# Conversion of float64 weights to float32 in a retention layer with two FFNs: the low word as an integer of 0 to 8, added to the high word's bits

## Chip, cores and metric

The kernel runs on one core of a Trainium2 chip. The metric is the device time of one launch in microseconds. The kernel before takes 1128.92 us, the median of three runs (1128.47 to 1130.82).

## What is computed

A retention layer over 4 x 8 heads, 768 tokens and 64 features, then an FFN with a quadratic gate, then an FFN whose two inputs are multiplied. The weights arrive as float64 and are used as float32.

```python
state = gamma * state + k_t v_t^T          # per head, 768 steps
x     = scale * q_t state                  # 3072 x 512 after all heads are laid side by side
h     = x @ w_in                           # 512 x 2048
g     = where(h >= 1, h, where(h <= -1, 0, (h + 1)**2 / 4))
x     = g @ w_out                          # 2048 x 512
out   = ((x @ w1) * (x @ w2)) @ w3 @ w_out2    # 512 x 1024, 512 x 1024, 1024 x 1024, 1024 x 512
```

## The kernel before

Tokens are worked on in 6 tiles of 512. The retention goes by 24 chunks of 128 tokens, each in four pieces (`piece_mm`, `piece_ew`): two of scores (`a_t`), one for the state, one for the output, which is split into `xh` and `xl`, the float32r halves that the first FFN reads. The first four chunks (16 pieces) run before the first FFN; the others run ahead of it, two pieces per slot at first, none in slots 7 to 18, then about one.

The first FFN has 96 slots (`SLOTS`), one for each token tile and block f of 128 hidden features. The first two tiles take the first half of the blocks, then the second half. A slot is `emit_h` (12 matmuls of 512 columns: high by high, low by high, high by low, over four blocks of the contraction), `emit_g1` (Relu and Square on ScalarE, a max-min on VectorE, into `r`), from slot 11 on `emit_g2` (split of `r` into `gh`, `gl`) and `emit_wo` (split of the `w_out` block into `wo_s`), and `emit_y1` one slot later. Slots 0 to 10 (`PLAIN`) use `r` and `wo_f` unsplit in plain float32. A split is a copy on ScalarE and a subtraction on VectorE (L96, L97). The product `w3 @ w_out2` and the second FFN follow; they read converted weights back from DRAM.

Weights are loaded as raw pairs of words (`load_job`, L118, on SP's DMA queue, 2 `raw` buffers), and become float32 in `converter`. `magnitude` (L155) takes the absolute value of the high word on ScalarE. VectorE then clamps it (L171), shifts it left by three and masks it (L176), puts sign and top exponent bit back (L181), masks the result to its power of two (L186), multiplies that by the low word and 2^-52 (L190), and adds the two (L202 for `w_in`, L218 for `w_out`, L229 for what is spilled to DRAM). The work list: `w_in` block 0 and 1 in 512 columns each, then ten conversions of 1024 columns (two blocks each, `w_out` and `w_in` in turn), then, from slot 10 on, ten of 512 columns for the rest of both, and forty of 512 columns whose result is stored to DRAM (`done_spill`).

The order on each engine is the program's order, as written. A planner decides where conversion steps stand: it books the time of each engine in `now`, with a cost for each step (the numbers that `converter` yields) and a due time for what VectorE does next. Where VectorE would wait for a matmul, `dve` puts in conversion steps until they would pass the due time, or until the weights that they need would not have arrived (`now["conv"]`). `magnitude` of the next conversion and the load of the one after it are issued when the generator is resumed after its fifth step, with the first step of `done`. SP's queue also carries the q, k and v loads (`chunk_ahead`) and the stores of converted weights, in program order.

Of the kernel before, what the change touches and what calls it, by code (L numbers as in the profile page):

```python
# [9 lines left out]
F32 = mybir.dt.float32  # L10
F32R = mybir.dt.float32r
U32 = mybir.dt.uint32
AF = mybir.ActivationFunctionType
ALU = mybir.AluOpType

B, H, S, D = 4, 8, 768, 64
P = 128
# [15 lines left out]
NB = NTILE * NF2  # L33
AHEAD = 6
HALF = NF1 // 2
# slots of the first FFN: the first two tiles take the weights in two halves, as they arrive
SLOTS = [(i, f) for lo in (0, HALF) for i in (0, 1) for f in range(lo, lo + HALF)]
SLOTS += [(i, f) for i in range(2, NTILE) for f in range(NF1)]
PLAIN = 11
# [10 lines left out]
def retention_then_two_ffns(  # L50
# [17 lines left out]
    nc = tc.nc  # L68
# [22 lines left out]
    cpool = conversion.enter_context(tc.tile_pool(name="cpool0", bufs=2))  # L91
# [9 lines left out]
        nc.tensor.matmul(out=ps, lhsT=ll, rhs=rh, start=False, stop=False)  # L101
        nc.tensor.matmul(out=ps, lhsT=lh, rhs=rl, start=False, stop=last)  # L102

# [1 line left out]
    win = {}  # L105
    wo = {}
    spill = {}
# [21 lines left out]
        return now["pe"]  # L129

    def dve(cost, after=0.0):
        """Counts a step of VectorE; weights are converted while it would wait."""
        while (jobs or conv is not None) and len(jobs) + 1 > now["hold"]:
            if conv is None:
                load_job(jobs[0])
                now["conv"] = max(now["conv"], ready[("raw", jobs[0][2])] + 1.1)
            start = max(now["dve"], now["conv"])
            if start + (0.2 if now["slip"] else 0.8) > after:
                break
            run_conv(1)  # L140
        now["dve"] = max(now["dve"], after) + cost
        return now["dve"]

    def dma(size, after=0.0):
        """When a load of so many KB arrives."""
        now["dma"] = max(now["dma"], after) + size / 350.0
        return now["dma"] + 1.9

    magnitudes = {}

    def magnitude(job):
        load_job(job)
        _, n, key, _ = job
        u = cpool.tile([P, n], U32, tag="u", name="u")
        nc.scalar.activation(out=u.bitcast(F32), in_=raws[key][:, 1::2].bitcast(F32), func=AF.Abs)  # L155
        magnitudes[key] = u
        now["conv"] = ready[("raw", key)] + 1.1

    def converter():
        """Yields the time of each step that holds VectorE."""  # L160
        while jobs:
            job = jobs.popleft()
            _, n, key, done = job
            if key not in magnitudes:
                magnitude(job)
            now["dve"] = max(now["dve"], now["conv"])
            raw, u = raws.pop(key), magnitudes.pop(key)
            lo, hi = raw[:, 0::2], raw[:, 1::2]
            w = cpool.tile([P, n], F32, tag="wf", name="w_f")
            uf, wu = u.bitcast(F32), w.bitcast(U32)  # L170
            nc.vector.tensor_scalar(  # L171
                out=uf, in0=uf, scalar1=bits(0x38000000), scalar2=bits(0x47F00000),
                op0=ALU.max, op1=ALU.min,
            )
            yield 0.2 + n / 1920
            nc.vector.tensor_scalar(  # L176
                out=u, in0=u, scalar1=3, scalar2=0x3FFFFFFF,
                op0=ALU.logical_shift_left, op1=ALU.bitwise_and,
            )
            yield 0.2 + n / 1920  # L180
            nc.vector.scalar_tensor_tensor(  # L181
                out=wu, in0=hi, scalar=0xC0000000, in1=u,
                op0=ALU.bitwise_and, op1=ALU.bitwise_or,
            )
            yield 0.2 + n / 960
            nc.vector.tensor_scalar(  # L186
                out=u, in0=wu, scalar1=0xFF800000, scalar2=None, op0=ALU.bitwise_and
            )
            yield 0.2 + n / 1920
            nc.vector.scalar_tensor_tensor(  # L190
                out=uf, in0=lo, scalar=2.0 ** -52, in1=uf, op0=ALU.mult, op1=ALU.mult
            )
            yield 0.2 + n / 960
            if jobs:
                magnitude(jobs[0])
            if len(jobs) > 1:
                load_job(jobs[1])
            yield from done(w, uf)

    def done_win(f):  # L200
        def done(w, u):
            nc.vector.tensor_tensor(out=w, in0=w, in1=u, op=ALU.add)  # L202
            yield 0.2 + w.shape[-1] / 960
            for i in range(w.shape[-1] // 512):
                t = new_w("win")
                split(t[:, 0, :], t[:, 1, :], w[:, i * 512:(i + 1) * 512])
                win[f + i] = t
                ready[("win", f + i)] = now["dve"] + 0.8
                yield 0.73

        return done

    def done_wo(f):
        def done(w, u):
            for i in range(w.shape[-1] // 512):
                t = wpool.tile([P, 512], F32, tag="wo", name="wo_f")
                c0 = i * 512
                nc.vector.tensor_tensor(  # L218
                    out=t, in0=w[:, c0:c0 + 512], in1=u[:, c0:c0 + 512], op=ALU.add
                )  # L220
                wo[f + i] = t
                ready[("wo", f + i)] = now["dve"] + 0.8
                yield 0.73

        return done

    def done_spill(key):
        def done(w, u):
            nc.vector.tensor_tensor(out=w, in0=w, in1=u, op=ALU.add)  # L229
            d = dram.tile([P, 512], F32, name=f"sp_{key[0]}_{key[1]}")  # L230
            nc.sync.dma_start(out=d, in_=w)
            spill[key] = d
            yield 0.73

        return done
# [17 lines left out]
        while jobs or conv is not None:  # L253
            run_conv(1)

# [1 line left out]
    stream = deque()  # L257
    arrived = deque()

# [6 lines left out]

    wos = {}

# [1 line left out]
    ch = {}  # L270
    vt = {}
    kt = {}
# [131 lines left out]
        )  # L404

    def chunk_ahead(a):
        """Loads where PE has long been done with what was there, so that no other load waits."""
        g, part = divmod(a, PIECES)
        if a < TILE_PIECES:
            if part == 0 and g:  # L410
# [11 lines left out]
        elif part == 2:  # L422
            scale_chunk(g + 1)

# [1 line left out]
    hps = {}  # L426
    gs = {}
    y1acc = {}
# [49 lines left out]
    y1_st = {}  # L478

    def group(n):  # L480
        """The slots that are summed up in PSUM together."""
        i, f = SLOTS[n]
        lo, hi = (0, NF1) if i > 1 else (0, HALF) if f < HALF else (HALF, NF1)
        return i, f == lo, f == hi - 1, hi < NF1, lo > 0
# [48 lines left out]
            nc.sync.dma_start(out=(y1_part if partial else y1_d)[i][m], in_=st)  # L533
        dve(2.2 if more else 0.8)

# [1 line left out]
    wo2 = {}  # L537
    w3 = {}
    wc = {}
# [29 lines left out]
            split(hi, lo, ps)  # L569
            wc[4 * hf + i] = (hi, lo)  # L570

# [1 line left out]
    wab = {}  # L573
    yt = {}
    abps = {}
# [62 lines left out]
    with tc.manual_schedule():  # L638
        for i in range(2):
            nc.gpsimd.memset(kp[i], 0.0)  # L640
            nc.gpsimd.memset(vp[i], 0.0)
        # in the order in which the slots want them
        order = [("win", w_in, 0, done_win)]
        for f in range(2, NF1, 2):
            order += [("wo", w_out, f - 2, done_wo), ("win", w_in, f, done_win)]
# [19 lines left out]
        load_job(jobs[0])  # L665
        load_v(1)

        # the first tile of tokens, while the first weights arrive
        early = [jobs[1]]
        for a in range(TILE_PIECES):  # L670
            piece_mm(a)
# [2 lines left out]
                load_job(early.pop(0))  # L674
            piece_ew(a)

        # first FFN; the retention runs ahead of it
        todo = deque(range(TILE_PIECES, NSTEP))
        now["slip"] = True
        for n in range(-1, NA):  # L680
# [92 lines left out]
            if hf:  # L773
                load_ab(NF2 + j)

        # second FFN
        for n in range(NB):
            i, f = divmod(n, NF2)
            if n + 1 < NB:
# [76 lines left out]
```

## Time and profile before

| | |
|---|---|
| median of three runs | 1128.92 us |
| lowest and highest run | 1128.47, 1130.82 us |
| span of the profiled execution | 1128.7 us |
| TensorE matmul (PE) busy | 1103.3 us, 98% |
| VectorE (DVE) busy | 630.1 us, 56% |
| ScalarE (ACT) busy | 390.7 us, 35% |
| GpSimd (POOL) busy | 69.4 us, 6% |

All times inside an execution are microseconds from the span's start. The releaser behind an arrow is what ended the idle time in front of an instruction. Matmuls overlap: their pace is the distance of their starts, not the duration of one. Busy shares are means over stages with different limits, so the page's totals are only the start; the rows further down are from windows and timelines of single stages.

### The profile page before, as it was taken

What the parts mean: (1) busy time and instruction counts of PE and PEld (TensorE: products, weight loads), DVE (VectorE), ACT (ScalarE), POOL (GpSimd) and SP (SyncE); (2) the same over time, 40 slices, a digit from 0 to 9 for tenths busy, and PEclk for the clock granted to TensorE, in tenths of its full rate; (3) what the DMA queues carried; (4) which work ended last, traced back from release to release, by engine and by line L of the source; (5) the groups of instructions that cost most, each with busy time, mean ns of one, the idle gap of its engine ahead of it and who ended that gap; (6) DMA issues with size and microseconds to landing.
All of it is one profiled execution on the core that took longest, in us unless ns stands there. A gap on an engine that the chain in (4) does not pass through costs nothing.

```text
span 1128.7 us, 13282 instructions
## 1 busy us (share of the span) xinstructions
PE 1103.3 (98%) x5268; PEld 916.0 (81%) x5268; DVE 630.1 (56%) x968; ACT 390.7 (35%) x657; POOL 69.4 (6%) x55
## 2 busy tenths in 40 slices
PE   6889999999999999999999999999999999999998
PEld 6666578888888888888888888888888888888887
DVE  5888778888989898887444454432221212122211
ACT  1223355434444544444334564421121212122111
POOL 3300100111011011010000000000000000000000
PEclk9899999999999999999999999999999999999999
DMA  7544225355544454353103123410101101010101
GB/s 207 178 159 152 90 94 172 99 185 179 177 150 150 137 170 160 131 160 111 38 1 131 47 84 112 137 60 1 66 10 45 30 1 66 1 38 0 38 1 38
DMA packets 56462, 107.37 MB, mean 95 GB/s; under 512 B 5584, under 2 KB 18000, under 8 KB 55120
## 3 DMA queue, kind: packets, MB, share of 16 engines
q1 hardware_dynamic: 56400, 106.52, 29.2%
q8 instruction: 41, 0.67, 0.3%
q14 instruction: 21, 0.17, 0.0%
HBM read 81.33 MB, written 25.17 MB: 94 GB/s over the span
## 4 chain that ended last, share of the span: by engine, by line
PE 93%; DVE 3%; DMA 2%; ACT 1%; POOL 1%; issue 0%; SPq 0%; POOLq 0%
PE hps L102 8%; PE hps L101 8%; PE ab L102 8%; PE ab L100 8%; PE ab L101 8%; PE hps L100 8%; PE y1acc L101 7%; PE y1acc L100 7%; PE y1acc L102 7%; PE oacc L629 4%; PE oacc L627 4%; PE oacc L628 4%; PE pa L339 3%; PE pa L359 3%; PE y1acc L501 2%; PE w3acc L100 1%
## 5 line engine op out<-in xcount | busy, mean ns | idle before, releaser
L612 DVE TENSOR_TENSOR pr<-ab,pr 128x512 f32<-128x512 f32 x48 | 33.2, 692 | 269.2 <-PE ab L102 269.2
L100 PE MATMUL hps<-xh,win 128*128 128x512 f32 x384 | 153.9, 401 | 6.6 <-ACT win L96 5.1
L102 PE MATMUL hps<-xl,win 128*128 128x512 f32 x384 | 151.7, 395 | 2.9 <-DVE xl L402 2.9
L101 PE MATMUL hps<-xh,win 128*128 128x512 f32 x384 | 151.5, 395 | 0.7 <-DVE win L97 0.7
L100 PE MATMUL ab<-yh,wab 128*128 128x512 f32 x384 | 149.4, 389 | 0.0
L101 PE MATMUL ab<-yh,wab 128*128 128x512 f32 x384 | 149.4, 389 | 0.0
L102 PE MATMUL ab<-yl,wab 128*128 128x512 f32 x384 | 149.4, 389 | 0.0
L100 PE MATMUL y1acc<-gh,wo_s 128*128 128x512 f32 x340 | 137.2, 404 | 0.0
L449 ACT ACTIVATE r<-hps 128x512 f32<-128x512 f32 x96 | 57.4, 598 | 229.1 <-PE hps L102 229.1
L101 PE MATMUL y1acc<-gh,wo_s 128*128 128x512 f32 x340 | 132.7, 390 | 0.0
L102 PE MATMUL y1acc<-gl,wo_s 128*128 128x512 f32 x340 | 132.5, 390 | 0.0
L451 DVE SCALAR_TENSOR_TENSOR r<-hps,r 128x512 f32<-128x512 f32 x96 | 66.3, 690 | 115.3 <-ACT r L450 115.0
L100 PEld LDWEIGHTS hps<-xh,win 128*128 128x128 f32 x384 | 73.4, 191 | 23.2 <-ACT win L96 5.6
L102 PEld LDWEIGHTS hps<-xl,win 128*128 128x128 f32 x384 | 73.3, 191 | 19.0 <-DVE xl L402 3.8
L101 PEld LDWEIGHTS hps<-xh,win 128*128 128x128 f32 x384 | 73.2, 191 | 17.4 <-DVE win L97 1.6
L611 ACT COPY pr<-ab 128x512 f32<-128x512 f32 x48 | 28.2, 587 | 170.8 <-PE ab L102 170.8
L101 PEld LDWEIGHTS ab<-yh,wab 128*128 128x128 f32 x384 | 72.1, 188 | 15.1
L102 PEld LDWEIGHTS ab<-yl,wab 128*128 128x128 f32 x384 | 72.1, 188 | 14.9
L100 PEld LDWEIGHTS ab<-yh,wab 128*128 128x128 f32 x384 | 72.1, 188 | 14.9
L96 ACT CAST ph<-pr 128x512 fp32r<-128x512 f32 x48 | 29.9, 622 | 138.2 <-DVE pr L612 138.2
L627 PE MATMUL oacc<-wch,ph 128*128 128x512 f32 x192 | 74.7, 389 | 0.0
L628 PE MATMUL oacc<-wcl,ph 128*128 128x512 f32 x192 | 74.7, 389 | 0.0
(71 smaller groups left out, 1789.5 us busy)
## 6 DMA issues: line engine op xcount, KB each, us to landing
raw<-in_w_dram SPq DMA_DIRECT2D x16, 512.0 KB, 3.9
raw<-in_w3t_dram SPq DMA_DIRECT2D x16, 512.0 KB, 3.7
raw<-in_w_out_dram SPq DMA_DIRECT2D x14, 512.0 KB, 4.0
q_t<-in_qT_dram SPq DMA_DIRECT2D x24, 256.0 KB, 4.9
kp<-in_kT_dram SPq DMA_DIRECT2D x48, 128.0 KB, 4.8
v_t<-in_v_dram SPq DMA_DIRECT2D x24, 256.0 KB, 4.4
y_d<-y1st SPq DMA_DIRECT2D x24, 256.0 KB, 2.6
f<-y_d SPq DMA_DIRECT2D x24, 256.0 KB, 2.7
```

Source lines behind the costliest of these rows:

```text
L96: nc.scalar.copy(out=hi, in_=src)
L100: nc.tensor.matmul(out=ps, lhsT=lh, rhs=rh, start=first, stop=False)
L101: nc.tensor.matmul(out=ps, lhsT=ll, rhs=rh, start=False, stop=False)
L102: nc.tensor.matmul(out=ps, lhsT=lh, rhs=rl, start=False, stop=last)
L339: nc.tensor.matmul(out=ps[:, j * C:(j + 1) * C], lhsT=kp[g % 2][:, h // 2, h % 2, :], rhs=q_t[:, h // 2, :], start=True, stop=True,)
L359: nc.tensor.matmul(out=y, lhsT=vb[:, p, h:h + 2, :], rhs=a_t[:, 2 * (p % 2) + h, :], start=(c == 0 and h == 0), stop=(h == 1),)
L449: nc.scalar.activation(out=r, in_=hps[n], func=AF.Relu, bias=0.5, scale=0.5)
L451: nc.vector.scalar_tensor_tensor(out=r, in0=hps.pop(n), scalar=1.0, in1=r, op0=ALU.max, op1=ALU.min)
L612: nc.vector.tensor_tensor(out=r, in0=pb, in1=r, op=ALU.mult)
L627: nc.tensor.matmul(out=ps, lhsT=lh, rhs=wh, start=(f == 0), stop=False)
L628: nc.tensor.matmul(out=ps, lhsT=lh, rhs=wl, start=False, stop=False)
L629: nc.tensor.matmul(out=ps, lhsT=ll, rhs=wh, start=False, stop=(f == NF2 - 1))
```

## The change

`magnitude` becomes `tail`: besides the absolute value of the high word, ScalarE writes the low word, scaled by 2^-29 through a Relu, as an unsigned integer of 0 to 8. VectorE adds this integer to the shifted high word, where the float product and its mask stood, and the and-or with the sign bits (`join`) becomes the last step, in `done`, in place of the float sum. The tile `w_f` is gone; the finished weight of a spilled conversion lies in `u`, whose bytes the store reads. `tail` of the next conversion and the load of the one after it are issued after the third step of a conversion, ahead of `join`. The planner's costs follow the steps. Comments and docstrings go too; such hunks are left out here.

```diff
-    magnitudes = {}
-
-    def magnitude(job):
+    tails = {}
+
+    def tail(job):
+
         load_job(job)
         _, n, key, _ = job
         u = cpool.tile([P, n], U32, tag="u", name="u")
         nc.scalar.activation(out=u.bitcast(F32), in_=raws[key][:, 1::2].bitcast(F32), func=AF.Abs)
-        magnitudes[key] = u
+        r = cpool.tile([P, n], U32, tag="r", name="r")
+        nc.scalar.activation(out=r, in_=raws[key][:, 0::2], func=AF.Relu, scale=2.0 ** -29)
+        tails[key] = (u, r)
         now["conv"] = ready[("raw", key)] + 1.1
...
-            if key not in magnitudes:
-                magnitude(job)
+            if key not in tails:
+                tail(job)
             now["dve"] = max(now["dve"], now["conv"])
-            raw, u = raws.pop(key), magnitudes.pop(key)
-            lo, hi = raw[:, 0::2], raw[:, 1::2]
-            w = cpool.tile([P, n], F32, tag="wf", name="w_f")
-            uf, wu = u.bitcast(F32), w.bitcast(U32)
+            raw, (u, r) = raws.pop(key), tails.pop(key)
+            hi = raw[:, 1::2]
+            uf = u.bitcast(F32)
...
             yield 0.2 + n / 1920
-            nc.vector.scalar_tensor_tensor(
-                out=wu, in0=hi, scalar=0xC0000000, in1=u,
-                op0=ALU.bitwise_and, op1=ALU.bitwise_or,
-            )
-            yield 0.2 + n / 960
-            nc.vector.tensor_scalar(
-                out=u, in0=wu, scalar1=0xFF800000, scalar2=None, op0=ALU.bitwise_and
-            )
-            yield 0.2 + n / 1920
-            nc.vector.scalar_tensor_tensor(
-                out=uf, in0=lo, scalar=2.0 ** -52, in1=uf, op0=ALU.mult, op1=ALU.mult
-            )
+            nc.vector.tensor_tensor(out=u, in0=u, in1=r, op=ALU.add)
             yield 0.2 + n / 960
             if jobs:
-                magnitude(jobs[0])
+                tail(jobs[0])
             if len(jobs) > 1:
                 load_job(jobs[1])
-            yield from done(w, uf)
+            yield from done(hi, u)
+
+    def join(out, hi, u):
+
+        nc.vector.scalar_tensor_tensor(
+            out=out.bitcast(U32), in0=hi, scalar=0xC0000000, in1=u,
+            op0=ALU.bitwise_and, op1=ALU.bitwise_or,
+        )
 
     def done_win(f):
-        def done(w, u):
-            nc.vector.tensor_tensor(out=w, in0=w, in1=u, op=ALU.add)
+        def done(hi, u):
+            w = u.bitcast(F32)
+            join(w, hi, u)
             yield 0.2 + w.shape[-1] / 960
...
     def done_wo(f):
-        def done(w, u):
-            for i in range(w.shape[-1] // 512):
+        def done(hi, u):
+            for i in range(u.shape[-1] // 512):
                 t = wpool.tile([P, 512], F32, tag="wo", name="wo_f")
                 c0 = i * 512
-                nc.vector.tensor_tensor(
-                    out=t, in0=w[:, c0:c0 + 512], in1=u[:, c0:c0 + 512], op=ALU.add
-                )
+                join(t, hi[:, c0:c0 + 512], u[:, c0:c0 + 512])
...
     def done_spill(key):
-        def done(w, u):
-            nc.vector.tensor_tensor(out=w, in0=w, in1=u, op=ALU.add)
+        def done(hi, u):
+            w = u.bitcast(F32)
+            join(w, hi, u)
             d = dram.tile([P, 512], F32, name=f"sp_{key[0]}_{key[1]}")
             nc.sync.dma_start(out=d, in_=w)
```

## Rows read from the trace of the kernel before

**Rows 1.** The page's first part: busy time, share of the span, instructions.

```profile
PE 1103.3 (98%) x5268; PEld 916.0 (81%) x5268; DVE 630.1 (56%) x968; ACT 390.7 (35%) x657; POOL 69.4 (6%) x55
```

**Rows 2.** Windows: length, each engine's busy time, granted clock, DMA share, GB/s.

```profile
0.00:40.00 40.00, 28.13 (x184) 26.85 (x184) 25.40 (x37) 6.68 (x10) 12.26 (x15) 0.91 0.73 220
40.00:125.00 85.00, 75.31 (x340) 54.03 (x341) 71.28 (x85) 25.18 (x37) 15.14 (x10) 0.94 0.44 145
...
200.00:520.00 320.00, 320.00 (x1706) 275.57 (x1705) 284.06 (x465) 146.02 (x248) 34.75 (x25) 1.00 0.48 155
...
1000.00:1128.70 128.70, 124.84 (x551) 103.07 (x549) 26.14 (x39) 22.89 (x39) 0.00 (x0) 1.00 0.07 25
```

**Rows 3.** Timeline of PE, 40 to 125: start, duration; idle and releaser in brackets.

```profile
43.02 0.79 PE L102 MATMUL hps<-xl,win 128*128 128x512 f32 x1 [2.10 <-DVE xl L402]
...
59.41 0.50 PE L100 MATMUL hps<-xh,win 128*128 128x512 f32 x1 [0.85 <-ACT win L96]
...
79.71 0.50 PE L100 MATMUL hps<-xh,win 128*128 128x512 f32 x1 [2.72 <-ACT win L96]
...
100.36 0.50 PE L100 MATMUL hps<-xh,win 128*128 128x512 f32 x1 [1.50 <-ACT win L96]
...
119.69 0.50 PE L100 MATMUL hps<-xh,win 128*128 128x512 f32 x1 [0.88 <-ACT xh L397]
...
121.21 0.76 PE L102 MATMUL hps<-xl,win 128*128 128x512 f32 x1 [0.79 <-DVE xl L402]
```

**Rows 4.** Chain of waits, 60 to 83: start, its share of the chain, link.

```profile
61.10 0.23 PE hps L101
...
75.80 1.96 DVE u L190
77.78 1.24 DVE w_f L202
...
82.08 0.43 PE hps L101
```

**Rows 5.** Groups of VectorE by shape: count, busy time, mean ns, idle before.

```profile
L190 DVE SCALAR_TENSOR_TENSOR u<-raw,u 128x512 f32<-128x512 uint32 x52 | 40.7, 783 | 1.5
...
L186 DVE TENSOR_SCALAR u<-w_f 128x512 uint32<-128x512 uint32 x52 | 23.0, 443 | 1.2
...
L190 DVE SCALAR_TENSOR_TENSOR u<-raw,u 128x1024 f32<-128x1024 uint32 x10 | 13.7, 1372 | 0.3
L181 DVE SCALAR_TENSOR_TENSOR w_f<-raw,u 128x1024 uint32<-128x1024 uint32 x10 | 12.2, 1223 | 0.2
...
L186 DVE TENSOR_SCALAR u<-w_f 128x1024 uint32<-128x1024 uint32 x10 | 8.3, 834 | 0.2
```

**Rows 6.** Groups of ScalarE by shape: the absolute value over 1024 columns.

```profile
L155 ACT ACTIVATE u<-raw 128x1024 f32<-128x1024 f32 x10 | 11.5, 1146 | 10.3 <-DMA raw<-in_w_out_dram 10.3
```

**Rows 7.** Tile `raw`: 145 to 525 (three rows), then landing from 0 to 145.

```profile
L155 ACT ACTIVATE u<-raw x50: 652/672/684, 147.0 to 517.7; 128x512 f32<-128x512 f32 x50
...
  ACT u L155: 13.3, 9
...
DMA to landing us min/median/max: 3.2/3.8/6.1
...
DMA to landing us min/median/max: 3.4/4.8/6.5
```

**Rows 8.** DMA issues, 140 to 520: count, size, median us to landing.

```profile
sp_wab<-w_f SPq DMA_DIRECT2D x16, 256.0 KB, 4.0
```

**Rows 9.** Timelines of DVE, ACT, DVE and PE around one slot, 302 to 314.

```profile
302.97 0.68 DVE L97 TENSOR_TENSOR wo_s<-wo_f,wo_s 128x512 fp32r<-128x512 f32 x1
...
306.07 0.60 ACT L449 ACTIVATE r<-hps 128x512 f32<-128x512 f32 x1 [2.53 <-PE hps L102]
...
309.36 0.68 DVE L97 TENSOR_TENSOR wo_s<-wo_f,wo_s 128x512 fp32r<-128x512 f32 x1
...
313.03 0.48 PE L100 MATMUL y1acc<-gh,wo_s 128*128 128x512 f32 x1
```

## The prediction

> **What bounds the kernel now.** I read the page's engine totals first: TensorE is busy for 1103.3 of 1128.7 us [rows 1]. So the change, which takes nothing from TensorE, can win only what TensorE idles, 25.4 us, and what it loses to a lower granted clock. The table of windows shows where that lies [rows 2]: 11.87 us before 40 us, 9.69 us from 40 to 125, 3.86 in the last output tile; the row from 200 to 520 has PE busy for its whole length, and the remaining windows are like it. VectorE, whose work the change cuts, is 84% busy in the second stretch and 89% from 200 to 520. In the latter it costs nothing, since PE never waits there. The stretch that decides is therefore 40 to 125.
>
> Next, PE's timeline of that stretch with its idle times [rows 3]. 2.10 at 43.02 waits for `xl`, the subtraction of the last piece of the first token tile. 0.85, 2.72 and 1.50 wait for the split of freshly converted `win` weights. 0.88 and 0.79 at 119.7 and 121.2 wait for the copy and the subtraction that finish the second token tile. These add up to 8.84; the other 0.85 are small pieces, most of them right behind the three `win` gaps, where the second half of the same split is late. Then the chain of waits [rows 4]: ahead of the 2.72 stand the converter's own steps on VectorE, L190 and L202. And the same fp32r matmul, 0.23 us apart at 61 us, is 0.43 apart at 82 us, after that gap: the windows' granted clock is 0.94 over this stretch against 1.00 later. The timeline has eight such matmuls after each of the idle times at 43.0, 79.7 and 121.2, so each costs 8 x 0.20 = 1.6 us beside its idle time.
>
> **What is removed from VectorE.** Per conversion of 1024 columns: the mask L186, 0.83, and the scaled product L190, 1.37 [rows 5]; of 512 columns 0.44 and 0.78. The old sum (L202, L218, L229) stays in number: its place is taken by `join`, the and-or of L181, and L181's place by the integer addition. So 2.2 us go per large conversion and 1.22 per small one. Two large conversions belong to each pair of f blocks, and the pairs come about 20.3 us apart (59.41, 79.71, 100.36). VectorE gets back 4.4 of each 20.3 us, where PE was short of 2.72 and 1.50. In 40 to 125 that is eight conversions, 17.6 of the 71.28 busy us.
>
> **What is added to VectorE.** An integer addition of two dense tensors does not occur before. Its nearest rows: L181, two 32-bit streams, one of them strided, 1.22 for 1024 columns, and the slowest L190, 1.96 while GpSimd multiplied [rows 4, 5]. I take 1.22, as it is nearest in kind; at 1.96 the saving per conversion falls from 2.2 to 1.5, still 3.0 per pair. Below 1.22 I see no ground: a two-stream f32 addition is not cheaper in any row.
>
> **What is added to ScalarE.** One more pass per conversion, over the low words. Abs over the other strided half takes 1.15 for 1024 columns and 0.67 for 512 [rows 6, 7]; I take the same for Relu, since both read one strided word and write a dense one. From integer words it might be a little longer; with 1.5 and 1.0 as the top nothing below changes. ScalarE is busy 25.18 of 85 us in the stretch and 146 of 320 later [rows 2], so the time itself is covered by idle time. Its place in the queue is not.
>
> The rule of the Trainium skill that speaks against this is in "ScalarE: Activation LUTs", section "Rules for kernel authors": relu, multiplications and additions belong on VectorE, which is faster per element. By it the low word would be one VectorE pass, an estimated 0.83 to 1.37 per conversion, and the gain per conversion would shrink from 2.2 to about 1. In this trace the strided ScalarE pass, 1.15, is no longer than L190, and ScalarE has the free time; the row decides for the change.
>
> **What moves.** `tail(jobs[0])` and `load_job(jobs[1])` come after the third step instead of the fifth, and *before* `join`, which is now the last reader of `raw`. The load of conversion k+2 reuses the buffer of k and therefore waits on SP's queue for join(k). So do the q, k and v loads and the spill store behind it; in the early stretch the converter as a whole is 2.2 us shorter, so they leave earlier than now. `u` now carries the finished weight, so Abs of k+2 must also wait for the spill store of k (4.0 us to land [rows 8]); before, only the third VectorE step of k+2 waited for such a store (in `wf`). ScalarE works in order: while that Abs waits, the first FFN's Relu, Square and splits stand behind it.
>
> **The sum, early stretch.** With 4.4 us back per pair the conversions of `win` run ahead of PE, so the three `win` gaps go: 0.85 + 2.72 + 1.50, plus 0.6 of the small pieces, plus the 1.6 of clock at 80 us. Even if VectorE kept its present order, the pair due at 59.4 would finish 2.2 us earlier. At 121 the subtraction would no longer stand behind late weights: 0.79 and 1.6 of clock go; the 0.88 for the copy, which can start only when the piece is done, stays. At 43.0, VectorE's queue ahead of `xl` is shorter, but `tail` may now hold ScalarE ahead of the copy `xh`; I take 0.5 of 2.10 and leave the clock. Before 40 us GpSimd and the q loads end last, not VectorE: 0, with +-0.7 for the same ScalarE order. Sum: 0.85 + 2.72 + 1.50 + 0.6 + 1.6 + 0.79 + 1.6 + 0.5 = 10.2 us.
>
> **The charge from 145 us on.** Here PE has no gap to win, and it can only get some. 50 small conversions take 371 us [rows 7], at 6.39 us a slot (the two `wo_s` rows, 302.97 and 309.36 [rows 9]) 0.86 per slot. The planner books 3.6 us for one now (three steps of 0.47, three of 0.73) and 2.4 after, so it will place about 1.25 per slot: in a quarter of some 40 slots two `tail`s fall into one VectorE stretch between `wo_s` and `r`. Then the second Abs waits. The stretch starts behind `wo_s` at 303.6, 2.5 us before h ends, which is where Relu starts, 306.07 [rows 9]. join(k) is done 0.7 later, the load is issued and lands 3.8 after [rows 7], the store at 4.0 plus 0.7 of queue; ScalarE then needs 0.67 twice. Relu of the slot would start 3.6 to 4.2 us after h's end instead of at once. From Relu to the last split takes 4.0 now (306.07 to 310.04), and y1 is due 7.0 after h's end (313.03, all [rows 9]). So such a slot stalls PE 0.6 to 1.2 us; where the pair lies earlier in the stretch, not at all. I take 0.3 for 10 slots, 3 us, between 0 and 12.
>
> The profiled span, 1128.7, is the median of the three runs, 1128.92, within 0.2 us, so nothing is to be added around it. 1128.9 - 10.2 + 3.0 = 1121.7 us.
>
> **The rivals.**
> - *No charge.* The planner spaces the loads well, or the slack of 3 us holds. For it: PE has no gap after 125 us although Abs already waits for loads there. 1118.7; with all 9.69 idle and 4.8 of clock won, 1114.4.
> - *Half the gain.* ScalarE, held ahead of `xh` by a `tail` that waits for its load (large loads land 4.8 after issue, up to 6.5 [rows 7]), makes new gaps of 2 to 3 us with their 1.6 of clock at the two tile starts. Against: the planner moves conversions away from there. -5 + 3: 1126.9.
> - *Slower.* The charge decides: same mechanism, but half of 40 slots pay the full 1.2 us, 24 us. 1128.9 - 10.2 + 24 = 1142.7. It turns the sign from 0.25 us per small conversion on. Against: it needs two tails in one stretch in every second slot, and the planner makes a conversion wait for its load.
> - *The change does not do what it says*: the new addition always runs at the slowest row, 1.96, and VectorE is relieved by a third less. A pair still gets 3.0 back against a gap of 2.72, so this costs some 1 us more: 1122.7.
>
> **How the numbers follow.** The forecast, 1119.5 to 1125, gets 0.50; no charge 0.23; half the gain 0.14; slower 0.11; nothing at all 0.02. The range takes in the first three and the unknown prices, and cuts the best end and the slower rival: 1116 to 1129. This kernel's measurement can tell 0.2% (2.3 us) from no change. Faster by more than that: forecast and no charge, 0.73. Within it: half the gain and nothing, 0.15. Slower: 0.12.
>
> **What would show it.** In the changed profile: no `win` gap over 0.5 us between 55 and 105 us; 0.23 us spacing at the matmuls that follow; VectorE busy in 40 to 125 near 54 us. For the charge: Abs waiting for `raw` or for a spill store for more than the 13.3 us of now [rows 7], and PE idle between 145 and 450 behind `gh` or `wo_s`, 0 to 12 us. The last small conversion starts near 400 us instead of 517.7. I am wrong if the gaps stay with VectorE idle before them (then a load or ScalarE holds the weights), or if PE idles after 145 us by more than 10 us.

## The result, and the profile after

The changed kernel takes 1145.3 us, the median of four runs (1140.77 to 1148.8), against 1128.81 for the kernel before in the same comparison: a ratio of 1.0135, 95% interval 1.0104 to 1.0166. It is slower by 1.35%, where 1121.7 and faster was forecast, and it lies above the range of 1116 to 1129. The profiled execution has a span of 1145.5 us.

Part 1 of the page and the windows of the changed kernel (length, then each engine's busy time, granted clock, DMA share, GB/s) answer to [rows 1, 2]:

```profile
PE 1110.5 (97%) x5268; PEld 918.5 (80%) x5268; DVE 547.5 (48%) x844; ACT 427.2 (37%) x719; POOL 65.1 (6%) x55
```

```profile
40.00:125.00 85.00, 77.83 (x362) 55.32 (x361) 63.38 (x81) 37.95 (x52) 13.96 (x10) 0.96 0.44 150
125.00:200.00 75.00, 73.08 (x307) 55.76 (x306) 49.32 (x86) 43.91 (x76) 0.00 (x0) 1.00 0.41 133
200.00:520.00 320.00, 309.90 (x1603) 263.69 (x1602) 221.08 (x354) 155.47 (x269) 32.20 (x24) 0.98 0.48 149
```

VectorE does get its relief, 547.5 us busy instead of 630.1. From 40 to 125 us TensorE is busy 2.5 us longer than before. But from 125 to 520, where it had no idle time at all, it now idles 1.92 + 10.10 = 12.0 us, and its granted clock falls.

To place the difference I use the start of the first ScalarE pass of a slot (the Relu that makes `r` from `hps`, from ScalarE's timeline) for slots 0, 11 and 81. The first stretch has most of the 1024-column conversions; the second has the 512-column ones.

| kernel | start to slot 0 | slots 0 to 11 | slots 11 to 81 |
|---|---|---|---|
| before | 47.08 | 96.85 | 463.78 |
| after | 45.04 | 94.20 | 485.35 |

So 2.65 us are won early and 21.6 lost late; behind slot 81 both are alike. Kernels whose program is the same up to slot 10 agree to 0.6 us from slot 0 to 11 (94.2 to 94.5 in the changed kernel, e1 and e5; 87.3 and 87.9 in e6 and e2). The time up to slot 0 is not used: it differs by 3.5 us (42.87 and 46.32) between e2 and e6, whose program is the same there.

TensorE's gaps in the changed kernel (timeline: start, duration, idle time and releaser in brackets), which answer to [rows 3]:

```profile
99.22 1.16 PE L337 MATMUL pa<-q_t,kp 128*128 128x128 f32 x8 [2.01 <-DVE xl L400]
...
113.89 0.50 PE L100 MATMUL hps<-xh,win 128*128 128x512 f32 x1 [3.65 <-ACT xh L395]
...
278.88 0.79 PE L100 MATMUL hps<-xh,win 128*128 128x512 f32 x1 [3.69 <-ACT xh L395]
...
308.08 0.50 PE L100 MATMUL y1acc<-gh,wo_s 128*128 128x512 f32 x1 [2.46 <-ACT wo_s L96]
308.88 0.75 PE L101 MATMUL y1acc<-gh,wo_s 128*128 128x512 f32 x1 [0.30 <-DVE wo_s L97]
309.43 0.63 PE L102 MATMUL y1acc<-gl,wo_s 128*128 128x512 f32 x1
309.86 0.63 PE L100 MATMUL y1acc<-gh,wo_s 128*128 128x512 f32 x1
```

The three gaps behind the split of `win` are gone. In their place stand gaps that lead to ScalarE: the copy `xh` at the tile starts (the 2.01 us at 99.22 wait for the subtraction `xl`, which stands behind an `xh` at 97.86), and from 150 us on also the split `wo_s`. Behind the gap at 308 us the matmuls start 0.43 us apart instead of 0.23, as after the gap at 80 us of the kernel before.

What ScalarE waits for in front of Abs, 125 to 520 us (total, times, longest); in the kernel before, Abs waited 13.7 us for `raw` there (13.3 from 145 to 525 [rows 7]) and never for a store:

```profile
ACT u L156 <- DMA sp_wab<-u: 31.3, 10, 8.3
ACT u L156 <- DMA sp_w<-u: 25.9, 14, 4.1
ACT u L156 <- DMA sp_wo<-u: 17.2, 7, 3.9
ACT u L156 <- DMA raw<-in_w_out_dram: 6.6, 4, 2.2
ACT u L156 <- DMA raw<-in_w_in_dram: 5.3, 2, 4.1
```

74.4 us behind spill stores. The longest wait, by the timelines of VectorE, GpSimd, SP's queue and ScalarE, around 300 us:

```profile
294.46 1.79 DVE L97 TENSOR_TENSOR wo_s<-wo_f,wo_s 128x512 fp32r<-128x512 f32 x1
296.17 1.53 DVE L193 SCALAR_TENSOR_TENSOR u<-raw,u 128x512 uint32<-128x512 uint32 x1
```

```profile
295.66 1.49 POOL L306 TENSOR_TENSOR vp<-v_t,small 128x512 f32<-128x512 f32 x1
```

```profile
297.76 0.34 SPq L118 DMA_DIRECT2D raw<-in_w_dram  x1
298.14 0.43 SPq L229 DMA_DIRECT2D sp_wab<-u  x1
```

```profile
294.81 0.65 ACT L158 ACTIVATE r<-raw 128x512 uint32<-128x512 uint32 x1
303.75 0.68 ACT L156 ACTIVATE u<-raw 128x512 f32<-128x512 f32 x1 [8.29 <-DMA sp_wab<-u]
304.32 0.66 ACT L158 ACTIVATE r<-raw 128x512 uint32<-128x512 uint32 x1
304.88 0.59 ACT L447 ACTIVATE r<-hps 128x512 f32<-128x512 f32 x1
```

Read it from the bottom. Relu (304.88) belongs to an h whose last matmul began at 297.10; it is some 7.4 us late, because two `tail`s precede it in ScalarE's order. The second one's Abs writes the `u` that the conversion two before it has just finished. So it waits until `join` (296.17, 1.53 long instead of 0.69 while GpSimd multiplies) is done, until SP has issued first the next load (297.76) and then the store (298.14), and until that store has landed, 5.6 us later.

### The profile page after: what moved, and what is told of

The parts are those of the page before. It is cut to its first block, busy times and chain, and to the rows that moved or that the text cites. A ratio compares the mean times of both kernels' runs of the same rounds, so it can differ in the third digit from the quotient of the medians.

```text
span 1145.5 us, 13272 instructions
## 1 busy us (share of the span) xinstructions
PE 1110.5 (97%) x5268; PEld 918.5 (80%) x5268; DVE 547.5 (48%) x844; ACT 427.2 (37%) x719; POOL 65.1 (6%) x55
## 4 chain that ended last, share of the span: by engine, by line
PE 75%; DMA 10%; DVE 8%; ACT 5%; issue 1%; SPq 1%; POOL 0%; ACTq 0%; POOLq 0%; DVEq 0%
PE ab L100 8%; PE ab L101 8%; PE ab L102 8%; PE hps L102 5%; PE hps L100 5%; PE hps L101 5%; PE y1acc L101 5%; PE y1acc L102 5%; PE y1acc L100 4%; PE oacc L625 4%; PE oacc L627 4%; PE oacc L626 4%; DMA sp_w<-u 3%; DMA sp_wab<-u 3%; PE pa L337 2%; PE pa L357 2%
## 5 line engine op out<-in xcount | busy, mean ns | idle before, releaser
L100 PE MATMUL y1acc<-gh,wo_s 128*128 128x512 f32 x340 | 138.5, 407 | 5.8 <-ACT wo_s L96 5.8
L101 PE MATMUL y1acc<-gh,wo_s 128*128 128x512 f32 x340 | 134.7, 396 | 1.8 <-DVE wo_s L97 1.8
L156 ACT ACTIVATE u<-raw 128x512 f32<-128x512 f32 (+1 forms) x62 | 46.5, 750 | 130.7 <-DMA sp_wab<-u 31.3
L102 PEld LDWEIGHTS ab<-yl,wab 128*128 128x128 f32 x384 | 72.1, 188 | 15.1
L100 PEld LDWEIGHTS y1acc<-gh,wo_s 128*128 128x128 f32 x340 | 64.9, 191 | 18.7 <-ACT wo_s L96 6.8
```

Of the source, the lines that this page charges most:

```text
L100: nc.tensor.matmul(out=ps, lhsT=lh, rhs=rh, start=first, stop=False)
```

## The experiments

In the table, "raw" and "store" are ScalarE's waits in front of Abs between 125 and 520 us, for loads and for spill stores; "0 to 11" and "11 to 81" are the stretches defined above. The ratio is to the kernel before as it was measured beside each run (medians from 1127.9 to 1131.0 us).

| kernel | median us | ratio to before, interval | 0 to 11 | 11 to 81 | raw | store |
|---|---|---|---|---|---|---|
| before | 1128.8 | | 96.9 | 463.8 | 13.7 | 0 |
| after | 1145.3 | 1.0135 (1.0104 to 1.0166) | 94.2 | 485.4 | 11.9 | 74.4 |
| e4_before_relu | 1129.7 | 0.9995 (0.9985 to 1.0004) | 97.6 | 463.8 | 15.1 | 0 |
| e2_old_pace | 1117.8 | 0.9899 (0.9875 to 0.9924) | 87.9 | 463.7 | 0.3 | 24.7 |
| e5_late_pace | 1125.9 | 0.9969 (0.9955 to 0.9983) | 94.5 | 463.9 | 1.2 | 32.0 |
| e6_early_pace | 1135.4 | 1.0064 (1.0042 to 1.0086) | 87.3 | 482.3 | 2.6 | 69.4 |
| e7_work_back | 1132.1 | 1.0038 (1.0017 to 1.0059) | 94.2 | 466.2 | 0.9 | 42.8 |
| e1_third_u | 1138.4 | 1.0080 (1.0058 to 1.0101) | 94.5 | 474.1 | 60.5 | 0 |
| e3_join_first | 1130.5 | 1.0011 (0.9998 to 1.0025) | 92.8 | 466.4 | 43.4 | 0 |
| e8_pace_join | 1127.5 | 0.9979 (0.9969 to 0.9989) | 91.7 | 464.4 | 1.5 | 0 |
| e9_third_raw | 1118.2 | 0.9886 (0.9864 to 0.9908) | 85.3 | 463.9 | 1.2 | 30.2 |
| e10_pace_third_raw | 1118.5 | 0.9897 (0.9870 to 0.9924) | 87.4 | 463.6 | 0.2 | 26.9 |
| e11_dense_third_raw | 1121.0 | 0.9938 (0.9915 to 0.9961) | 85.3 | 468.2 | 0 | 23.1 |
| e12_raw_join | 1122.7 | 0.9950 (0.9933 to 0.9967) | 85.3 | 466.0 | 46.8 | 0 |

### Is it the extra ScalarE pass? (e4_before_relu)

The kernel before with the Relu pass added; nobody reads what it writes.

```diff
         nc.scalar.activation(out=u.bitcast(F32), in_=raws[key][:, 1::2].bitcast(F32), func=AF.Abs)
+        r = cpool.tile([P, n], mybir.dt.uint8, tag="r", name="r", bufs=1)
+        nc.scalar.activation(out=r, in_=raws[key][:, 0::2], func=AF.Relu, scale=2.0 ** -29)
```

> The kernel before with one more ScalarE pass per conversion, the Relu of the low words, written to a byte tile that nothing reads: the ScalarE work of the change alone, with the old order, pace and VectorE work. Theories S and O: 0.67 us per small conversion is covered, 1128 to 1131, PE idle from 200 to 520 under 0.5. Rival A (the extra pass itself holds ScalarE's queue): above 1134.

The time and the late stretch don't change; the early one is 0.75 us longer in the profiled run. The pass itself costs nothing here; its place and what it waits for are another matter.

### Is it the pace of the conversions? (e2, e5, e6, e7)

The planner books 1.2 us less for a conversion of 512 columns and 2.0 less for one of 1024, and so sets them closer. In the program order of the changed kernel 12 of the slots from 11 on have two `tail`s between one slot's Relu and the next; in that of the kernel before 3 have. e2_old_pace books the two dropped steps without doing them:

```diff
             nc.vector.tensor_tensor(out=u, in0=u, in1=r, op=ALU.add)
             yield 0.2 + n / 960
+            yield 0.2 + n / 1920
+            yield 0.2 + n / 960
```

> The changed kernel, but the planner books 0.47 and 0.73 us more per small conversion (the two steps that are gone), so that it places the conversions at about the pace of before. Theory S with pace as the trigger (two tails in one stretch make the second wait for the store): the last conversion again starts near 515 us, waits for stores under 20 us, PE idle from 200 to 520 under 2 us, time 1120 to 1127. Rival O (the store and the load are simply in front of ScalarE's queue whatever the pace, because tail and load now stand ahead of join): still above 1138.

The windows of e2_old_pace:

```profile
40.00:125.00 85.00, 82.47 (x382) 58.28 (x381) 60.69 (x79) 39.10 (x53) 13.29 (x10) 1.00 0.46 155
200.00:520.00 320.00, 320.00 (x1704) 275.58 (x1704) 233.23 (x375) 166.16 (x285) 34.32 (x26) 1.00 0.50 156
```

1117.8 us, faster than both kernels: 9.0 us are won early and nothing is lost late. Every operation of the change is in it, so the 27.5 us to the changed kernel are due to order alone. e5_late_pace books so only from slot 10 on (below); e6_early_pace, with `if not late_pool`, only up to there:

```diff
+            if late_pool:
+                yield 0.2 + n / 1920
+                yield 0.2 + n / 960
...
                 cpool = conversion.enter_context(tc.tile_pool(name="cpool1", bufs=2))
+                late_pool = True
```

> The changed kernel with the two dropped steps booked again from slot 10 on only (small conversions); the first twelve conversions at the new pace. Theory T (the dense pace costs in both stretches, and the two are separate): the early stretch as in the changed kernel, 4 to 5 us ahead of before at slot 11, no loss later: 1123 to 1127. Rival E (the later stalls follow from where the early stretch leaves the conversions): above 1132.

> The changed kernel with the two dropped steps booked again for the first twelve conversions only. Theory T: 13 us ahead of before at slot 11, as with the old pace throughout, then 15 to 22 us lost between slots 11 and 55: 1131 to 1139. Rival E: no loss later, under 1122.

The two halves come apart: e5 has the early stretch of the changed kernel (94.5) and the late one of the kernel before (463.9), e6 the reverse (87.3 and 482.3). The dense pace costs in both: some 18.5 to 21.6 us late, and early 6.3 to 6.9 of the 9 that the same work wins at the old pace.

e7_work_back keeps the old pace and fills the booked time again with a mask and a scaled product, whose result nobody needs:

```diff
+            nc.vector.tensor_scalar(
+                out=r, in0=r, scalar1=0xFF800000, scalar2=None, op0=ALU.bitwise_and
+            )
             yield 0.2 + n / 1920
+            nc.vector.scalar_tensor_tensor(
+                out=r.bitcast(F32), in0=raw[:, 0::2], scalar=2.0 ** -52, in1=r.bitcast(F32),
+                op0=ALU.mult, op1=ALU.mult,
+            )
```

> The changed kernel with two VectorE instructions put behind the addition, of the kinds and sizes that the change took away (a mask and a scaled product with the low word, written to r, which nothing reads after that) and booked as before. Order of tail and load, ScalarE work and store into u stay as changed. Theory V (the 13 us that the old pace brings are VectorE's saved work): the gaps ahead of win come back, 1128 to 1133. Rival (they come from the new order, or from tails standing elsewhere in ScalarE's queue): below 1122.

The early gain shrinks from 9.0 to 2.7 and the gaps behind the split of `win` are back (1.94 at 79.9, 2.01 at 99.6 us). So the gain comes from VectorE's saved work, as predicted.

### Store or load? (e1, e3, e8)

e1_third_u gives `u` a third buffer from slot 10 on; the room for it is taken from `r`, which has one there.

```diff
-        u = cpool.tile([P, n], U32, tag="u", name="u")
+        u = cpool.tile([P, n], U32, tag="u", name="u", bufs=3 if late_pool else 2)
...
-        r = cpool.tile([P, n], U32, tag="r", name="r")
+        r = cpool.tile([P, n], U32, tag="r", name="r", bufs=1 if late_pool else 2)
```

> The changed kernel, but from slot 10 on with three u buffers and one r buffer in place of two and two (the same bytes): the absolute value of conversion k+2 no longer has to wait for the store of k, which reads u. Theory S (the charge comes from ScalarE standing behind the store of a finished weight in u): the 74 us that ScalarE waits for stores between 145 and 525 fall under 5, PE's idle time between 200 and 520 falls from 10.1 to under 2, its granted clock there returns to 1.00, and the 18.9 us lost between slots 27 and 55 go: 1125 to 1129. Rival P (the pace of the conversions, or their loads, hold ScalarE just as long): ScalarE waits for raw instead, the time stays above 1138.

The median, 1138.4, lies at the bound of rival P (above 1138) and not in theory S's 1125 to 1129, yet half of the loss comes back: the waits for stores are gone, and 11.2 of 21.6 us with them. In their place Abs waits for loads, 60.5 us, the two longest rows being (125 to 520 us):

```profile
ACT u L157 <- DMA raw<-in_w_dram: 23.7, 13, 4.3
ACT u L157 <- DMA raw<-in_w3t_dram: 18.5, 15, 2.9
```

The single `r` adds 24.9 us of short waits of its own, in front of the Relu pass, so the 10.4 that stay are not all the loads'.

e3_join_first puts `tail` and the next load behind `join`; e8_pace_join does the same to e2_old_pace.

```diff
+            steps = done(hi, u)
+            yield next(steps)
             if jobs:
                 tail(jobs[0])
             if len(jobs) > 1:
                 load_job(jobs[1])
-            yield from done(hi, u)
+            yield from steps
```

> The changed kernel, but tail of the next conversion and the load after it are issued behind the first join, as in the order of before, where they came after the last read of raw. Rival O: the load no longer waits on SP's queue for join, ScalarE's waits fall under 20 us, time 1120 to 1128. Theory S: the store of k is still issued less than one conversion before the absolute value of k+2 wants u; waits for stores stay above 40 us, time above 1136.

> The changed kernel at the old pace, and with tail and load behind the first join. If the position ahead of join still costs anything at the old pace, the 1.5 us gap at 72 us or ScalarE's remaining waits for stores (25 us) shrink, 1115.5 to 1117; if not, 1117 to 1119, the same as at the old pace alone.

e3 fits neither of its theories (1120 to 1128, or above 1136): it takes 1130.5. The late loss is down to 2.6 us though Abs still waits 43.4 us for loads: behind `join`, fewer second `tail`s stand ahead of a Relu (8 slots instead of 12), and the spill store now goes ahead of the load. e8 missed its expectation by some 8 us: late it is within 0.7 us of e2, but 3.8 of the early 9 us are lost again, with a gap of 3.21 for `win` at 97 us; the rest of its distance to e2, 5.2 us, lies ahead of slot 0. The gap at 97 us comes from the `tail` that is issued later and not from a late load. ScalarE's timeline of e8 ahead of that `win`:

```profile
93.95 0.59 ACT L399 CAST xh<-pa 128x512 fp32r<-128x512 f32 x1 [4.85 <-PE pa L361]
94.43 1.12 ACT L156 ACTIVATE u<-raw 128x1024 f32<-128x1024 f32 x1
95.45 1.12 ACT L158 ACTIVATE r<-raw 128x1024 uint32<-128x1024 uint32 x1
96.45 1.14 ACT L96 CAST win<-u 128x512 fp32r<-128x512 f32 x2
```

Abs doesn't wait for its words there. The cast of `win`, whose `join` began at 90.34 and took 1.22 us, stands in program order behind `xh`, which waits for TensorE, and behind the two passes of `tail`.

### What eats the early gain, and what the store waits for (e9 to e12)

e9_third_raw is e5 (old pace late, dense early) with three `raw` buffers up to slot 10; Relu writes in place, which makes the room.

```diff
-            raw = cpool.tile([P, 2 * n], U32, tag="raw", name="raw")
+            raw = cpool.tile([P, 2 * n], U32, tag="raw", name="raw", bufs=2 if late_pool else 3)
...
-        r = cpool.tile([P, n], U32, tag="r", name="r")
-        nc.scalar.activation(out=r, in_=raws[key][:, 0::2], func=AF.Relu, scale=2.0 ** -29)
+        r = raws[key][:, 0::2]
+        nc.scalar.activation(out=r, in_=r, func=AF.Relu, scale=2.0 ** -29)
```

> The changed kernel with the old pace of conversions from slot 10 on, as in the run that kept the dense pace early only, and with three raw buffers instead of two up to slot 10; to make room the Relu pass writes its integers in place over the low words, and the tile for them is gone. Open is what eats 5 to 6.5 of the 9 us that the old pace gains in slots 0 to 11. Theory L: ScalarE stands at an Abs pass whose raw words have not arrived (7.56 us at 95.82 us of the changed kernel), with the cast that makes xh behind it; a third buffer starts each load one conversion earlier. Then slots 0 to 11, on ScalarE from one first-half-of-Square pass to the other, take 91 us or less (94.5 with the dense pace), the gap of about 2 us near 100 us is gone, and the median is 1121 to 1124. Theory W: the casts of win wait for VectorE's join (7.79 us at 112.22 us) and xh stands behind those; a buffer more changes nothing of that. Then slots 0 to 11 take over 93 us, a wait of 3 to 4 us for xh near 115 us stays, and the median is 1125 to 1127.

The place in question, on ScalarE's timeline, in the changed kernel:

```profile
95.82 1.14 ACT L156 ACTIVATE u<-raw 128x1024 f32<-128x1024 f32 x1 [7.56 <-DMA raw<-in_w_out_dram]
96.85 1.11 ACT L158 ACTIVATE r<-raw 128x1024 uint32<-128x1024 uint32 x1
97.86 0.59 ACT L395 CAST xh<-pa 128x512 fp32r<-128x512 f32 x1
...
112.22 1.14 ACT L96 CAST win<-u 128x512 fp32r<-128x512 f32 x2 [7.79 <-DVE u L193]
113.26 0.58 ACT L395 CAST xh<-pa 128x512 fp32r<-128x512 f32 x1
```

With the third buffer both waits are gone, also the one behind the `win` cast, because a conversion that gets its words in time ends in time. Slots 0 to 11 take 85.3 us, 11.6 less than before, and the median is 1118.2. That is better than the load theory had expected (91 and 1121), and against its rival. That the Relu pass now writes in place has no part in it: in the changed kernel that pass never waited for its tile. Its rows of the changed kernel (count, busy time, mean ns, idle before):

```profile
L158 ACT ACTIVATE r<-raw 128x1024 uint32<-128x1024 uint32 x10 | 11.3, 1132 | 0.0
...
L158 ACT ACTIVATE r<-raw 128x512 uint32<-128x512 uint32 x52 | 34.5, 663 | 0.0
```

TensorE's only idle time from 45 to 520 us in e9 is

```profile
109.46 0.50 PE L101 MATMUL hps<-xh,win 128*128 128x512 f32 x1 [0.68 <-ACT xh L399]
```

e10_pace_third_raw adds the same buffers to e2_old_pace.

> The changed kernel with the old pace of conversions throughout (the kernel that took 1117.8 us), with the same Relu pass in place and three raw buffers up to slot 10. Theory L: what is left idle on TensorE between 60 and 115 us there (0.3 to 1.2 us in three places) comes from loads of raw words as well: slots 0 to 11 take 86 to 87.5 us instead of 87.9, and the median is 1115.5 to 1117. Theory W: no load is late there, the median is 1117 to 1119. If loads into a third buffer take the DMA engines from the loads of x and wo early on, it is slower than 1119.

Nothing is gained (1118.5 against 1117.8, as theory W had it), though slots 0 to 11 take 87.4 us against 87.9, which lies in theory L's range. One load was late at the old pace: in e2 Abs waits 2.24 us for `raw` at 68.58 us, and with the third buffer this wait is gone. But TensorE's 1.19 us ahead of `win` (at 72.35 in e2, 75.48 in e10) stay: that `win` stands behind an `xh` that waits for TensorE.

e11_dense_third_raw is the changed kernel with its own dense pace throughout and three `raw` buffers in both stages; `u` keeps its two.

```diff
+            raw = cpool.tile([P, 2 * n], U32, tag="raw", name="raw", bufs=3)
```

> The changed kernel with its own dense pace throughout, the Relu pass in place over the low words, and three raw buffers in both stages; u keeps its two buffers, so an Abs pass still stands behind the store of the conversion two before. The counterpart of the run with a third u. Early (slots 0 to 11) as in the run with three raw buffers and the old pace late: 85 to 88 us. Late (slots 11 to 81, 485.4 in the changed kernel, 463.8 before): Theory S, the store is the wait that ends last and the load would have come in time behind it: 10 us or less come back, 475 to 484, the waits of Abs for stores stay at 60 us or more, median 1125 to 1136. Rival R, the loads set the pace as well and the two add up: 470 to 476, median 1121 to 1126. Rival Q, the stalls come from dense VectorE work and not from ScalarE's queue: late stays at 483 to 486, with either wait away.

A miss for all three theories: 17.2 of the 21.6 us come back, more than any of them had, with ScalarE's program order as it was, 12 double `tail`s among it, and with no buffer added for the stores. The waits for stores fall from 74.4 to 23.1 us by themselves. Tile `u` between 145 and 525 us shows what changed with them; the changed kernel first, then e11:

```profile
L229 SPq DMA_DIRECT2D sp_w<-u x16: 327/432/433, 355.0 to 440.4; - x16
...
  ACT u L156: 74.4, 31
...
DMA to landing us min/median/max: 2.0/4.2/6.7
```

```profile
L229 SPq DMA_DIRECT2D sp_w<-u x16: 326/327/376, 330.5 to 412.9; - x16
...
  ACT u L156: 24.1, 12
...
DMA to landing us min/median/max: 2.0/2.1/5.8
```

The same store of 256 KB lands in 2.1 us instead of 4.2. With two buffers the load of conversion k+2 and the store of k wait for the same `join(k)`, and SP issues them 0.4 us apart, the 512 KB load first (297.76 and 298.14 above). With three, that load no longer waits for `join(k)`: it leaves right behind the store of the conversion before, and the store of k goes alone. SP's queue in e11:

```profile
261.22 0.38 SPq L118 DMA_DIRECT2D raw<-in_w_dram  x1
264.69 0.33 SPq L229 DMA_DIRECT2D sp_wab<-u  x1
...
294.57 0.33 SPq L229 DMA_DIRECT2D sp_wab<-u  x1
294.99 0.38 SPq L118 DMA_DIRECT2D raw<-in_w_dram  x1
```

The other runs agree: the median landing of these stores is 4.2 to 4.3 us in the eight kernels with the load right ahead of the store (after, e1, e2, e5, e6, e7, e9, e10), and 2.1 to 2.2 in the four where it is not (e3, e8, e11, e12). In "DMA: Bandwidth & Descriptors", section "Two DMAs through the same engine are not ordered", the Trainium skill says that descriptors of one queue on one DMA engine start in order but need not complete in order; that a store starts behind the load ahead of it agrees with these 2 us. A mere sharing of the engines by the two transfers fits less well: in e3, e8 and e12 the load is mostly issued 0.4 us behind the store, and the store still lands in 2.1 to 2.2 us. How the 17.2 us divide between the shorter landing and the loads that leave earlier isn't shown, since in e11 both come with the one buffer.

e12_raw_join has e11's buffers and e3's order.

> The same three raw buffers and dense pace, and besides the passes of the next conversion and the load after it come behind join, as in the earlier run with join first, so that neither the store nor the load should be waited for. If the waits at the head of ScalarE's queue are the whole late charge: slots 11 to 81 take 463.8 to 466 us and the sum of waits of Abs between 125 and 520 us is under 25 us; with an early stretch of 85 to 92 the median is 1116 to 1124. If dense VectorE work alone costs something: 468 or more with those waits gone.

The late stretch is within 2.2 us of the kernel before, and the early one is again 85.3. But Abs still waits 46.8 us for loads, where under 25 was expected:

```profile
ACT u L156 <- DMA raw<-in_w3t_dram: 22.6, 10, 3.6
ACT u L156 <- DMA raw<-in_w_dram: 22.2, 11, 3.5
```

So the sum of these waits doesn't set the cost: 46.8 us of them go with a loss of 2.2 here, 60.5 with 10.4 in e1. What counts is whether something is due behind them; 8 double slots instead of 12 fit that, but no run changes their number alone. The fastest are e2, e9 and e10, 1.0 to 1.1% below the kernel before; their intervals do not part them.

## Why the prediction was wrong

**What bounds the kernel, and the early sum (-10.2).** The mechanism was right, and the size too, but not in this kernel. With the loads in time the early stretch gains 11.6 us (e9, e11, e12), at the old pace 9.0 and 9.5 (e2, e6); with the work put back 2.7. In the changed kernel the three `win` gaps go as said, 5.07 us, and new ones of 2.01 and 3.65 us come ahead of and at the second tile's start. So 2.65 us are won from slot 0 to 11, where the sum had 9.7 (its 0.5 at 43 us lies ahead of slot 0). That is the rival "half the gain" in kind ("new gaps of 2 to 3 us with their 1.6 of clock at the two tile starts"), at one tile start of the two, and with about half of the 5 us that it had left. Its argument against, that the planner moves conversions away from there, did not hold.

**The prices of single operations.** Right. Relu over the low words takes 663 ns for 512 columns and 1132 for 1024 (assumed: as Abs, 0.67 and 1.15). The addition, which had no row, takes about what L181 took:

```profile
L183 DVE CUSTOM_DVE_ANT_0 u<-u,r 128x1024 uint16<-128x1024 uint16 x52 | 37.4, 720 | 2.6
...
L183 DVE CUSTOM_DVE_ANT_0 u<-u,r 128x2048 uint16<-128x2048 uint16 x10 | 12.7, 1268 | 0.2
```

1.27 for 1024 columns against 1.22 assumed. The rule of the Trainium skill that was weighed ("ScalarE: Activation LUTs", "Rules for kernel authors": such work belongs on VectorE, with a speed that the page gives for bf16) was rightly set aside: e4 shows that the ScalarE pass over these 32-bit words costs nothing by itself. No run put the low word on VectorE.

**What moves.** This step failed. It named everything that went wrong: the load waits for `join(k)`, the store is queued behind it, Abs waits for that store, ScalarE works in order. But it priced the first two at nothing ("in the early stretch the converter as a whole is 2.2 us shorter, so they leave earlier than now") and took the 4.0 us landing of the store [rows 8] as a property of the store. It was the landing of a store with a load ahead of it, 0.7 us or more in the kernel before. And it checked only whether the load leaves earlier than before, not whether it leaves early enough for a converter that now needs its words sooner.

**The charge (+3.0, bound 12).** The mechanism held, and so did the count: 12 double slots where 10 were forecast. The price did not: 0.3 us a slot was taken, 1.2 given as the most, and 21.6 / 12 = 1.8 is the measured mean. Slot by slot it is no such price. TensorE idles at seven places, slots 23, 25 and 27 cost nothing though they are double, and by the starts of the slots' first matmuls 16.0 of the 21.6 us are lost between slots 31 and 38, where slots 31, 33 and 35 are double. There ScalarE is still late from one slot when the next is due: slot 35's Relu (309.07) starts 5.2 us late with no wait in front of its own `tail`. The sum had priced each slot by itself, and only behind `gh` and `wo_s`; 4.36 of the 12.0 us of idle time are waits for `xh` at tile starts (278.88 and 399.73), which it didn't have. Three terms were too small. In the slot shown above Relu started 7.4 us after its h, not 3.6 to 4.2: `join` and the subtraction ahead of it took 1.53 and 1.79 instead of 0.69 each beside GpSimd (1.9 us), and the store landed 5.6 us after its issue, not 4.0 (1.6 us). And the clock was left out, though the sum for the early stretch had counted 1.6 us of it per gap. TensorE's idle time late is 12.0 us; that this is the upper bound is luck, as it is made up otherwise. The other 9.6 us of 21.6 are mostly the clock. By windows of the changed kernel:

```profile
260.00:280.00 20.00, 16.31 (x82) 13.40 (x81) 13.50 (x22) 11.11 (x20) 3.07 (x2) 0.96 0.71 216
280.00:300.00 20.00, 20.00 (x91) 16.82 (x90) 16.56 (x26) 7.13 (x12) 3.26 (x2) 0.87 0.46 139
300.00:320.00 20.00, 17.24 (x80) 14.16 (x80) 11.58 (x21) 8.60 (x15) 0.00 (x0) 0.91 0.55 176
320.00:340.00 20.00, 17.88 (x84) 14.66 (x83) 15.41 (x24) 10.47 (x18) 2.62 (x2) 0.91 0.42 123
```

0.04, 0.13, 0.09 and 0.09 of 20 us each are an estimated 7.0 us in these 80 alone, 6.4 if only TensorE's busy time is taken. The window from 280 to 300, right behind the gap of 3.69 us, has no idle time of TensorE and still loses 2.6.

**The rivals.** The kernel took the way of "slower" (1142.7, given 0.11), with "half the gain" on top of it; I had treated the two as alternatives. They have one cause, the dense pace with loads and stores that wait for `join`, and so came together. By the profiled spans: 1128.7 - 4.7 (2.0 up to slot 0, which is within the 3.5 that this time varies by, and 2.65 behind it) + 21.6 = 1145.6, against 1145.5. That "slower" comes near the time is in part luck: it had 20 slots at 1.2 us and no clock.

**What would show it.** No `win` gap between 55 and 105: right, and near 82 us the matmuls start 0.23 us apart. VectorE near 54 us from 40 to 125: 63.4, since the stretch now holds nine large additions where it held eight scaled products, and TensorE is further on in its slots. The last small conversion near 400: its Abs starts at 432.1. Abs waiting for stores was the sign named for the charge, TensorE idle late by more than 10 us the one for being wrong, and both came.

**Readings to put right.** The prediction set the profiled span of 1128.7 equal to the median time. A run's time is longer than its span, by 2.0 us in the changed kernel (1147.54 and 1145.5), so by this margin the profiled execution before is the slowest of its three runs, 1130.82, and not the median. This changes no term of the sum.

## What to carry to other kernels

When work is taken off an engine that feeds a pipeline, ask first who sets the pace of that pipeline: here a planner packed the steps closer, and an engine that works in order then stood at the head of its queue, for a DMA, ahead of work that was due. A buffer that is released by the last step of a conversion ties its next load and its store to one moment; one buffer more for the load was worth 24 us here (1145.3 to 1121.0, ratios 1.0135 and 0.9938 to the kernel before), where a third buffer for the tile that the store reads (e1, from slot 10 on) brought 7. A stall on the path of TensorE has to be priced with the clock that is lost behind it.

## What was not expected of the hardware

- A store of 256 KB lands in 2.1 us, and in 4.2 with a 512 KB load issued 0.4 us ahead of it on the same queue (medians over the stores of one run). With the load 0.4 us behind the store it is 2.1 to 2.2 again.
- The addition of two tiles of 32-bit integers is one instruction on VectorE, shown as an operation on twice as many 16-bit elements, and takes 0.72 us for 512 columns, as long as the and-or of the same tiles (0.75).
- In e12 ScalarE stands 46.8 us at loads and TensorE loses at most 2.2 us by it; in the changed kernel it stands 74.4 us at stores and 21.6 are lost.
